# A state-space scan with top-1 experts on one core: the second layer of the rows beyond 256 with the weights standing still

## The chip, the cores and the metric

The kernel runs on one core of a Trainium2 chip. The metric is device time in microseconds of one execution, the median over runs. The engines are TensorE (PE, with its weight loads shown apart as PEld), VectorE (DVE), ScalarE (ACT), GpSimd (POOL) and SyncE (SP), which here only issues DMAs. "PEq" or "PEldq" is the sequencer of TensorE: it takes instructions in order and hands them to the array. TensorE multiplies a standing operand (lhsT, loaded by a weight load) with a moving one (rhs), and writes to PSUM.

## The reference

Two blocks in a row. The first is a chunked state-space scan (mamba2) over 4 batches x 8 heads x 768 steps; its output, seen as 3072 tokens x 256 features, goes to a mixture of 8 experts, one for each token:

```python
logits = x @ w_gate                      # x (3072, 256), w_gate (256, 8)
expert_idx = np.argmax(logits, axis=1)
probs = softmax(logits);  gate_w = probs[np.arange(N), expert_idx]
for e in range(8):
    mask = expert_idx == e
    h = np.maximum(x[mask] @ w1[e], 0.0)         # w1[e] (256, 1024)
    out[mask] = gate_w[mask, None] * (h @ w2[e]) # w2[e] (1024, 256)
```

Everything is float32. How many tokens an expert gets is known only at run time.

## The kernel before, in words

**Scan and placing (to about 65 us).** The scan makes a row of 320 numbers for each token (its 256 features, and parts of the gate's logits) and the token's number. GpSimd writes each row to a place of its own in `x_hbm`, a region of rows for each expert, with indirect DMAs (`place`, L434). The last group of 8 blocks of tokens is placed while the first expert jobs already run (`more_places`, L878).

**Jobs.** `jobs` (L479) is a list of pieces of expert work. Pass 0 is the first P1 = 256 rows of experts 0 to 3, pass 1 the next P2 = 192 rows of the same experts, pass 2 all 448 rows of experts 4 to 7. Rows that no token fills are zero and point to no token. `m_load` (L482) fetches a job's rows on the SP queue, four DMAs for the features and one or more for the rest of the row (`lt`, and `lh` for the half tile below). `m_xT` (L523) turns the features with a DVE transpose (`xT`, or `xTw` for pass 2) and works out the gate factors (`gates`, L502), which takes seven small DVE operations and one exponential on ACT between them.

**First layer.** `up` (L554) holds a 128x128 piece of w1 as the standing operand and moves the rows' features through it: 8 pieces f x 2 pieces t, n columns each, into one of four PSUM buffers `h_ps`. ACT applies ReLU and writes `hT` (1024 hidden features by rows; two such buffers).

**Second layer.** `m_y` (L589) works by tiles of 128 rows: the piece of `hT` is the standing operand and 256 columns of w2 move, 8 matmuls a tile, into one of two PSUM buffers `y_ps`. `put` (L575) multiplies by the gate (ACT for the first jobs, DVE from job 3 on) and GpSimd sends the 128 rows to their tokens in `out` with an indirect DMA (`send`, L570).

**Pairs.** Passes 1 and 2 run in pairs of experts (`m_pair`, L627). The number of rows n of a pair is known at run time: DVE counts the tokens (`over`, L451), and PE and ACT load the number of the size as a register (`number_of`, L619). `tc.Switch` (L634) then jumps to one of 17 programs, each written for one n: from 128 to 192 in steps of 4 for pass 1, from 320 to 448 in steps of 8 for pass 2. A program holds both experts' first layers, and `m_half` (L602): of the rows beyond 128 (pass 1) or 384 (pass 2), up to 64 of each expert side by side in one tile, 256 columns of w2 moving; where there are none, a product with zero on ACT. `tc.switch_hint` (L927, L942) tells the sequencers of PE and ACT ahead of time which program comes.

**Order.** It is written out by hand (`manual_schedule`): jobs 0 to 3, each first layer then second layer; then for each of four pairs the program, the hint for the next pair, the transposes and gates of the next pair, and the second layers of both. Weights of experts 0 to 2 have places of their own, 3 to 5 others that come free after the scan, and experts 6 and 7 take the places of 0 and 1. They are loaded on SP by `load_w` (L206) in quarters of 256 KB, at points of this order (`between`, `last_weights`, L883 and L934); two small DMAs (`go`, L599) make SP wait for a finished tile before it goes on to the later loads.

Of the kernel before, what the change touches and what calls it, by code (L numbers as in the profile page):

```python
# [41 lines left out]
MG = 7  # L42
PASS = ((0, P1, 2), (P1, P2, 1), (0, P1 + P2, 3))
WSIZES = list(range(P1 + FEW, P1 + P2 + 1, 8))
NR = N + 512
EW = 3
# [5 lines left out]
def ssd_then_moe(ctx, tc, xs_in, ae_in, wgx, w_gate, w1, w2, gx, gb, gc, ga, out):  # L52
# [42 lines left out]
    go = route.tile([1, 1], FP32, name="go")  # L95
# [68 lines left out]
    def empty_consts():  # L164
# [4 lines left out]
        for hT in hT_all:  # L169
            nc.gpsimd.memset(hT[:, :, WSIZES[0]:P1 + 128], 0.0)  # L170
# [308 lines left out]
    jobs = [(p, e) for p in range(2) for e in range(HE)] + [(2, e) for e in range(HE, E)]  # L479
    ex = [dict() for _ in jobs]  # L480

    def m_load(i, engs=(nc.sync,)):  # L482
# [4 lines left out]
        xb = mo.tile([128, (n if p == 2 else P1) // 32 * 64], FP32, name="xw" if p == 2 else "xb", bufs=2 if p == 2 else 4)  # L487
# [4 lines left out]
        lt = mo.tile([128, 3, MID], FP32, name="lt", bufs=7)[:, 0:tiles]  # L492
        nc.sync.dma_start(out=lt, in_=x_hbm[r0:r0 + 128 * tiles, DM:W].rearrange("(t p) w -> p t w", p=128))
        ex[i]["lt"] = lt
        if p and e % 2 == 0:
            lh = mo.tile([128, 1, MID], FP32, name="lh", bufs=3)
            for u in range(2):
                q = r0 + u * NR + 128 * tiles
                nc.sync.dma_start(out=lh[64 * u:64 * u + 64, 0], in_=x_hbm[q:q + 64, DM:W])
            ex[i]["lh"] = ex[i + 1]["lh"] = lh  # L500

    def gates(mids):  # L502

        ns = [m.shape[1] for m in mids]
        n = sum(ns)
        at = [sum(ns[:k]) for k in range(len(ns))]
        sh = [128, n, E]
        l = mo.tile([128, MG, E], FP32, name="t_l", bufs=2)[:, 0:n]
        for m, o, k in zip(mids, at, ns):
            logits(l[:, o:o + k], m)  # L510
        mx = mo.tile([128, MG], FP32, name="t_mx", bufs=2)[:, 0:n]
        nc.vector.tensor_reduce(mx, l, axis=AX, op=ALU.max)
        sub = mo.tile([128, MG, E], FP32, name="t_sub", bufs=2)[:, 0:n]
        nc.vector.tensor_tensor(out=sub, in0=l, in1=bc(mx[:, :, None], sh), op=ALU.subtract)
        nc.scalar.activation(sub, sub, func=ACT.Exp)  # L515
        se = mo.tile([128, MG], FP32, name="t_se", bufs=2)[:, 0:n]
        nc.vector.tensor_reduce(se, sub, axis=AX, op=ALU.add)  # L517
        nc.vector.tensor_scalar(out=se, in0=se, scalar1=1e-9, scalar2=None, op0=ALU.add)
        gt = mo.tile([128, MG], FP32, name="t_gt", bufs=5)[:, 0:n]
# [3 lines left out]
    def m_xT(i):  # L523
        p, e = jobs[i]
        n = PASS[p][1]
        for j in range(i, i + (2 if p else 1)):
            ex[j]["xT"] = (mo.tile([128, KT, n], FP32, name="xTw", bufs=2) if p == 2 else
                           mo.tile([128, KT, P1], FP32, name="xT", bufs=4))
            nc.vector.transpose(ex[j]["xT"][:, :, 0:n].rearrange("p k (r j) -> p k r j", j=32), ex[j]["xb"])  # L529
        if p:  # L530
            ex[i]["g"], ex[i + 1]["g"], ex[i]["gh"] = gates([ex[i]["lt"], ex[i + 1]["lt"], ex[i]["lh"]])
# [17 lines left out]

    def y_next():  # L550
        turn_no[1] += 1
        return Y[turn_no[1] % 2][:, 0:DM]
# [36 lines left out]
    def m_y(i, pp, then=None):  # L589
        e = jobs[i][1]  # L590
        for t in range(PASS[jobs[i][0]][2]):
# [5 lines left out]
            if then and (i < HE or t == 0):  # L597
                if i >= HE:
                    nc.sync.dma_start(out=go, in_=ex[i]["yo"][0:1, 0:1])  # L599
                then()  # L600
# [411 lines left out]
```

## Time and profile before

| what | us |
|---|---|
| median of 3 runs | 252.14 (251.94 to 254.53) |
| the profiled execution | 252.34 |
| its span, first to last instruction | 250.6 |
| PE busy | 237.7 |
| PEld busy | 185.7 |
| DVE, ACT, POOL busy | 82.5, 82.3, 75.4 |
| first-layer job of 256 rows on PE, start to start | 6.9 |
| second layer of one tile of 128 rows on PE | 3.45 |
| one half tile in a pair's program | 3.6 |
| one indirect send on POOL | 0.98 |

The difference between the profiled execution's own time and its span is what lies around the first and the last instruction. The granted TensorE clock is 0.999 throughout. In the rows of the profile, L558 is the first layer, L594 the second layer by tiles, L612 the half tile, L640 ReLU in a pair's program, L567 ReLU elsewhere, L578 the gate product on DVE, L571 the indirect send, L529 the transpose of a job's rows. A float32 matmul of the source appears as two matmul instructions, each with its weight load.

### The profile page before, as it was taken

The numbers are of one execution on the slowest core, as the hardware profiler recorded it, in microseconds if no ns is written. First come the engines' busy times: TensorE is split into PE (matmuls) and PEld (weight loads), VectorE is DVE, ScalarE is ACT, GpSimd is POOL, SyncE is SP. The second block draws the span as 40 slices with busy tenths as digits, with TensorE's granted clock in tenths as the row PEclk, the third lists the DMA queues.
The fourth block names the chain that finished last, engine by engine and source line by source line (L and its number), as shares of the span: only waits on it lengthen the run. The fifth ranks groups of instructions, "written<-read, shape, count | busy, mean of one in ns | idle before, by whom it ended". The sixth has DMA issues, their size and how long they took to land. (4 is left out here: it accounts for less than half of the span.)

```text
span 250.6 us, 5147 instructions
## 1 busy us (share of the span) xinstructions
PE 237.7 (95%) x1893; PEld 185.7 (74%) x1893; DVE 82.5 (33%) x220; ACT 82.3 (33%) x259; POOL 75.4 (30%) x129
## 2 busy tenths in 40 slices
PE   7898999987799999999999999999999999999992
PEld 4676877665588888888898978666788755558881
DVE  5897879677632123104121501010311100000110
ACT  4666657792131322324061431233300033420000
POOL 3664787673004833030113102100133200003331
PEclk9999999999999999999999999999999999999999
DMA  6999997724899437597971100640059600001101
GB/s 169 359 354 340 336 306 240 263 86 110 221 323 385 148 104 160 129 284 212 269 172 28 47 3 19 146 96 3 5 170 352 251 20 0 0 3 34 44 24 44
DMA packets 36363, 39.23 MB, mean 157 GB/s; under 512 B 21519, under 2 KB 24018, under 8 KB 36308
## 3 DMA queue, kind: packets, MB, share of 16 engines
q1 hardware_dynamic: 33156, 31.10, 41.6%
q0 software_dynamic: 2496, 7.28, 8.0%
q8 instruction: 27, 0.44, 0.8%
q10 hardware_dynamic: 656, 0.18, 0.3%
q14 instruction: 28, 0.23, 0.3%
HBM read 29.72 MB, written 9.35 MB: 156 GB/s over the span
## 5 line engine op out<-in xcount | busy, mean ns | idle before, releaser
L594 PE MATMUL y_ps<-w,hT 128*128 128x256 f32 x384 | 84.7, 380 | 0.0
L594 PEld LDWEIGHTS y_ps<-w,hT 128*128 128x128 f32 x384 | 72.6, 190 | 11.0 <-issue 0.8
L640 ACT ACTIVATE hT<-h_ps 128x128 f32<-128x128 f32 (+3 forms) x64 | 25.3, 395 | 66.5 <-PE h_ps L558 66.2
L558 PE MATMUL h_ps<-xT,w 128*128 128x256 f32 (+2 forms) x256 | 45.2, 335 | 1.2 <-DVE xT L529 1.2
L571 POOL DMA_INDIRECT out_dram<-yo,lt x24 | 23.7, 986 | 71.1 <-DVE yo L578 41.3
L558 PEld LDWEIGHTS h_ps<-xT,w 128*128 128x128 f32 x256 | 40.3, 190 | 4.9 <-DVE xT L529 1.5
L558 PE MATMUL h_ps<-xTw,w 128*128 128x368 f32 (+1 forms) x128 | 42.5, 492 | 0.0
L558 PEld LDWEIGHTS h_ps<-xTw,w 128*128 128x128 f32 x128 | 24.3, 190 | 17.4 <-issue 9.9
L578 DVE TENSOR_SCALAR yo<-y_ps,t_gt 128x256 f32<-128x256 f32 x18 | 8.7, 481 | 71.1 <-PE y_ps L594 71.1
L286 DVE TENSOR_TENSOR M<-g,mask 128x1024 f32<-128x1024 f32 x24 | 28.2, 1219 | 7.6 <-PE g L281 5.8
L425 POOL DMA_INDIRECT x_hbm<-rows,pos x24 | 23.9, 996 | 12.4 <-DVE pos L412 4.6
L571 POOL DMA_INDIRECT out_dram<-yh,lh x4 | 3.9, 984 | 62.1 <-ACT yh L614 36.6
L567 ACT ACTIVATE hT<-h_ps 128x256 f32<-128x256 f32 x32 | 12.1, 385 | 19.3 <-PE h_ps L558 12.9
L339 PE MATMUL y<-M,xp 128*32 128x128 f32 x384 | 15.5, 277 | 2.7 <-DVE M L286 2.2
L281 PE MATMUL g<-cm,xs_n 32*128 32x256 f32 x192 | 15.9, 405 | 1.3 <-issue 1.3
L517 DVE TENSOR_REDUCE t_se<-t_sub 128x2 f32<-128x16 f32 (+2 forms) x8 | 1.5, 182 | 44.2 <-ACT t_sub L515 44.2
L351 PE MATMUL r<-turn,yT 128*128 128x160 f32 x88 | 14.9, 312 | 1.2 <-ACT yT L344 1.0
L265 ACT ACTIVATE cm<-xs_n,par 128x128 f32<-128x128 f32 x46 | 15.1, 417 | 2.6 <-DMA xs_n<-in_xs_dram 2.5
L351 PEld LDWEIGHTS r<-turn,yT 128*128 128x128 f32 x88 | 12.2, 189 | 4.9 <-ACT yT L344 3.9
L344 ACT COPY yT<-y 128x512 f32<-128x512 f32 x12 | 7.0, 586 | 21.6 <-PE y L339 16.5
L275 POOL TENSOR_TENSOR xp<-xs_n,Ei 128x256 f32<-128x256 f32 x20 | 12.1, 619 | 5.4 <-DVE xp L275 3.4
L281 PEld LDWEIGHTS g<-cm,xs_n 32*128 32x128 f32 x192 | 9.5, 185 | 5.2 <-issue 4.8
(124 smaller groups left out, 149.7 us busy)
## 6 DMA issues: line engine op xcount, KB each, us to landing
w<-in_w_dram SPq DMA_DIRECT2D x64, 256.0 KB
xs_n<-in_xs_dram SPq DMA_DIRECT2D x20, 320.0 KB
xw<-x_hbm SPq DMA_DIRECT2D x16, 112.0 KB
x_hbm<-zrows SPq DMA_DIRECT2D x1, 1344.0 KB
xb<-x_hbm SPq DMA_DIRECT2D x14, 64.0 KB
xs_n<-in_xs_dram SPq DMA_DIRECT2D x4, 192.0 KB
xb<-x_hbm SPq DMA_DIRECT2D x16, 48.0 KB
xs_n<-in_xs_dram SPq DMA_DIRECT2D x4, 128.0 KB
```

Source lines behind the costliest of these rows:

```text
L265: nc.scalar.mul(t[:, u], st[n]["CT"], par[:, u:u + 1])
L275: eng.tensor_tensor(out=t, in0=st[n]["x"].rearrange("p (h d) -> p h d", d=D), in1=bc(Ei[:, n, :, None], [128, NH, D]), op=ALU.mult)
L281: nc.tensor.matmul(g_ps[:, q, n % 2], lhsT=st[n]["BT"][r], rhs=st[n]["cm"][r].rearrange("p u i -> p (u i)"), start=True, stop=True)
L286: nc.vector.tensor_tensor(out=t, in0=g_ps[:, :, n % 2].rearrange("p q (u i) -> p q u i", u=2), in1=bc(mask[:, None, None, :], [128, 4, 2, ...
L339: nc.tensor.matmul(y_ps[o:o + D, h // 4, CH * s:CH * s + CH], lhsT=st[n]["xp"][:, D * h:D * h + D], rhs=st[n]["M"][:, h], start=first, sto ...
L351: nc.tensor.matmul((to[s] if to else r_ps[:, s])[:, 256 * t:256 * t + 160], lhsT=sd[d]["yT"][:, t, CH * s:CH * s + CH], rhs=turn[:, t].rea ...
L425: s_ = nc.gpsimd.indirect_dma_start(out=x_hbm[:, :], out_offset=bass.IndirectOffsetOnAxis(ap=at, axis=0), in_=row, in_offset=None)
L558: nc.tensor.matmul(p[:, 0:n], lhsT=w[:, c:c + 128], rhs=xT[:, t, 0:n], start=(t == 0), stop=(t == KT - 1))
L567: nc.scalar.activation(ex[i]["hT"][:, f, 0:n], q, func=ACT.Relu)
L571: return nc.gpsimd.indirect_dma_start(out=out[:, :], out_offset=bass.IndirectOffsetOnAxis(ap=tok, axis=0), in_=yo[:, :], in_offset=None, b ...
L594: nc.tensor.matmul(p, lhsT=ex[i]["hT"][:, f, 128 * t:128 * t + 128], rhs=w_sb[e][1][:, f * DM:f * DM + DM], start=(f == 0), stop=(f == FT ...
L640: nc.scalar.activation(ex[i + u]["hT"][:, f, 0:n], q, func=ACT.Relu)
```

## The change

The rows beyond 256 get their second layer the other way round: a 128x128 piece of w2 stands (every second output column, so that a piece is 128 of the 256 features) and the n (pass 1) or n - 256 (pass 2) columns of `hT` move. This is done inside the pair's program (`m_rest`), so that n is exact, into a whole PSUM buffer for each expert. The result has features on partitions. `rest_out` turns it with DVE in blocks of 32x32, writes it to a table in memory with four DMAs an expert, and reads it back as two tiles of 96 rows; `rest_put` multiplies by the gate on GpSimd and sends them. The half tile, the zeroing of `hT` for it, and the pass 1 tiles are gone; pass 2 has two tiles by `m_y` instead of three. There is a third `hT` buffer. The jobs' order is new: (0,0), (0,1), (0,2), pair (1,0)+(1,1), the first layer of (0,3), pair (1,2)+(1,3), the second layer of (0,3), then the two pairs of pass 2. Loads, hints and weights are placed anew; the `go` DMAs are gone.

```diff
-PASS = ((0, P1, 2), (P1, P2, 1), (0, P1 + P2, 3))
+PASS = ((0, P1, 2), (P1, P2, 0), (0, P1 + P2, 2))
+REST = ((0, 0), (0, P2), (P1, P1 + P2))
+HP = P2 // 2
...
-        for hT in hT_all:
-            nc.gpsimd.memset(hT[:, :, WSIZES[0]:P1 + 128], 0.0)
...
+        if p:
+            lr = mo2.tile([HP, 2, MID], FP32, name="lr", bufs=6)
+            q = e * NR + P1
+            nc.sync.dma_start(out=lr, in_=x_hbm[q:q + P2, DM:W].rearrange("(t p) w -> p t w", p=HP))
...
+            if p == 2:
+                ex[i]["g"], ex[i + 1]["g"] = gates([ex[i]["lt"], ex[i + 1]["lt"]])
+            ex[i]["gr"], ex[i + 1]["gr"] = gates([ex[i]["lr"], ex[i + 1]["lr"]])
...
+    def m_rest(i, n):
+        p, e = jobs[i]
+        a = REST[p][0]
+        for f in range(2 * FT):
+            k, f = divmod(f, FT)
+            w = w_sb[e][1][:, f * DM:f * DM + DM].rearrange("p (m k) -> p k m", k=2)
+            nc.tensor.matmul(ex[i]["yr"][:, P2 * k:P2 * k + n - a], lhsT=w[:, k], rhs=ex[i]["hT"][:, f, a:n],
+                             start=(f == 0), stop=(f == FT - 1), skip_group_check=True)
+
+    def rest_out(i):
+        for j in range(i, i + 2):
+            t = mo2.tile([128, P2 // 32, 32, 2], FP32, name="rT", bufs=2)
+            nc.vector.transpose(t.rearrange("p r i k -> p k r i"),
+                                ex[j]["yr"][:, 0:2 * P2].rearrange("p (k r j) -> p k r j", k=2, j=32))
+            y = ys_hbm[jobs[j][1]]
+            for c in range(4):
+                nc.sync.dma_start(out=y[:, 64 * c:64 * c + 64].rearrange("(r j) z -> j r z", j=32),
+                                  in_=t[32 * c:32 * c + 32].rearrange("p r i k -> p r (i k)"))
+        for j in range(i, i + 2):
+            t = mo2.tile([HP, 2, DM], FP32, name="ys", bufs=2)
+            nc.sync.dma_start(out=t, in_=ys_hbm[jobs[j][1]].rearrange("(t p) w -> p t w", p=HP))
+            ex[j]["ys"] = t
+
+    def rest_put(i):
+        for j in range(i, i + 2):
+            for t in range(2):
+                yo = mo2.tile([HP, DM], FP32, name="yp", bufs=2)
+                nc.gpsimd.tensor_scalar(out=yo, in0=ex[j]["ys"][:, t], scalar1=ex[j]["gr"][:, t:t + 1], scalar2=None,
+                                        op0=ALU.mult)
+                put_out(yo, ex[j]["lr"][:, t])
...
             for u in range(2):
                 for f in range(FT):
                     q = up(ex[i + u]["xT"], w_sb[e + u][0], f, n, pp)
                     nc.scalar.activation(ex[i + u]["hT"][:, f, 0:n], q, func=ACT.Relu)
-            m_half(i, n, yo)
+            for u in range(2):
+                m_rest(i + u, n)
...
+        first(2)
+        hint(0)
+        m_y(2, pp)
+        m_xT(5)
+        m_pair(3, pp)
+        for j in (8, 9):
+            m_load(j)
+        rest_out(3)
+        first(5)
+        hint(1)
+        rest_put(3)
+        m_pair(6, pp)
+        hint(2)
+        rest_out(6)
+        m_xT(8)
+        m_y(5, pp)
+        rest_put(6)
+        m_pair(8, pp)
+        hint(3)
+        for j in (10, 11):
+            m_load(j)
+        m_xT(10)
+        rest_out(8)
+        for k in range(16):
+            load_w(E - 2 + k // 8, k % 8 // 4, k % 4)
+        m_y(8, pp)
+        rest_put(8)
+        m_y(9, pp)
+        m_pair(10, pp)
+        rest_out(10)
+        m_y(10, pp)
+        rest_put(10)
+        m_y(11, pp)
```

In the new list of jobs, 0 to 2 are (0,0) to (0,2), 3 and 4 are (1,0) and (1,1), 5 is (0,3), 6 and 7 are (1,2) and (1,3), and 8 to 11 are experts 4 to 7. The weights of expert 4 and half of expert 5's are loaded during job 1, before the rows of jobs 5 to 7, the other half of expert 5's during job 5.

## The prediction

> **What bounds the kernel now.** I read the page's busy table first, then PE in order of time, then the instructions at each jump, then the last microseconds of all engines.
>
> ```profile
> span 250.6 us, 5147 instructions
> PE 237.7 (95%) x1893; PEld 185.7 (74%) x1893; DVE 82.5 (33%) x220; ACT 82.3 (33%) x259; POOL 75.4 (30%) x129
> ```
>
> PE is the bound: no other engine passes a third. So the change is worth what it takes off PE's line, less any hole it makes there, less what it adds after PE's last matmul. PE from the third first-layer job on (start, length, line, shape, count):
>
> ```profile
> 110.68 7.07 PE L558 MATMUL h_ps<-xT,w 128*128 128x256 f32 x32
> 117.59 7.07 PE L594 MATMUL y_ps<-w,hT 128*128 128x256 f32 x32
> 124.49 7.31 PE L558 MATMUL h_ps<-xT,w 128*128 128x128 f32 x64
> 131.64 7.07 PE L594 MATMUL y_ps<-w,hT 128*128 128x256 f32 x32
> 138.56 9.16 PE L558 MATMUL h_ps<-xT,w 128*128 128x164 f32 x64
> 147.65 3.65 PE L612 MATMUL y_ps<-w,hT 128*36 128x256 f32 x32
> 151.23 7.17 PE L594 MATMUL y_ps<-w,hT 128*128 128x256 f32 x32
> 158.24 19.95 PE L558 MATMUL h_ps<-xTw,w 128*128 128x368 f32 x64
> 178.03 20.88 PE L594 MATMUL y_ps<-w,hT 128*128 128x256 f32 x96
> 198.75 22.51 PE L558 MATMUL h_ps<-xTw,w 128*128 128x416 f32 x64
> 221.19 3.65 PE L612 MATMUL y_ps<-w,hT 128*32 128x256 f32 x32
> 224.76 20.99 PE L594 MATMUL y_ps<-w,hT 128*128 128x256 f32 x96
> ```
>
> Each row starts where the one before stops: no holes, not even at the jumps. The shapes also tell which programs this data picks: n = 128, 164, 368, 416 for the four pairs; two pairs (128 and 368) have no 64-row half at all. A matmul in the source is two instructions (x32 for 16). I use start to start, since the lengths overlap: 7.15/64 = 0.1117 us for 128 columns, 9.09/64 = 0.1420 for 164, 19.79/64 = 0.3092 for 368, 22.44/64 = 0.3506 for 416, 6.91/32 = 0.216 for 256; a line of 0.00083 us a column.
>
> The jump into the second pair's program (PE's and ACT's hint, PE's jump, first instruction of the program):
>
> ```profile
> L942 PEldq BRANCH_PREFETCH_HINT  x1: 31/31/31, 131.4 to 131.4; - x1
> L942 ACTq BRANCH_PREFETCH_HINT  x1: 31/31/31, 134.8 to 134.8; - x1
> ...
> L1007 PEldq COMPARE_BRANCH  x2: 413/1929/3445, 130.4 to 135.0; - x2
> ...
> L634 ACTq BRANCH_PREFETCH_HINT  x1: 36/36/36, 137.8 to 137.8; - x1
> L634 PEldq BRANCH_PREFETCH_HINT  x1: 45/45/45, 138.5 to 138.5; - x1
> ```
>
> PE's jump at 135.0 took 3445 ns and the program began at 138.5, 7.0 us after the hint. It cost nothing because PE's sequencer was 3.6 us ahead of its array, whose next matmul was due at 138.56. It is a hidden stall with 0.1 us to spare.
>
> The end:
>
> ```profile
> 242.34 0.48 DVE L578 TENSOR_SCALAR yo<-y_ps,t_gt 128x256 f32<-128x256 f32 x1 [2.97 <-PE y_ps L594]
> 243.10 0.98 POOL L571 DMA_INDIRECT out_dram<-yo,lt  x1 [1.99 <-DVE yo L578]
> 245.79 0.48 DVE L578 TENSOR_SCALAR yo<-y_ps,t_gt 128x256 f32<-128x256 f32 x1 [2.97 <-PE y_ps L594]
> 246.55 0.98 POOL L571 DMA_INDIRECT out_dram<-yo,lt  x1 [2.47 <-DVEq L946]
> ```
>
> POOL is idle 2 us before each send, so the last send leaves at once: 0.76 us after the put starts, and the span ends 4.05 us after the send starts.
>
> **The change, part by part.** The profiled execution took 252.34 us, with a span of 250.6; the 1.7 around it I leave. The median of the three runs is 252.14, 0.2 below.
>
> *Matmuls removed.* Pairs 1 and 2 lose their 256-column second halves: 6.92 (131.64 to 138.56) and 7.01. Pairs 3 and 4 lose the third of three tiles: 20.72/3 = 6.91 and 6.90. The halves: 3.58 and 3.57. Sum 34.9 us.
>
> *Matmuls added.* 64 instructions a pair (2 experts x 8 x 2, doubled), of n columns in pairs 1 and 2, n - 256 in pairs 3 and 4: 128, 164, 112, 160. That is 64 x 0.1117 = 7.15, 64 x 0.1420 = 9.09, 64 x 0.1383 (the line at 160) = 8.85. For 112 the line says 0.0984, but its weight load is as large as in the 128-column row, where PEld is busy without a pause (7.10 of 7.10 us in that window), so I take that row: 7.15 (6.30 as the low end). Sum 32.2 us (31.4). **Net on PE: -2.65 us** (-3.5). Rows became columns, but only pairs 2 and 4 had much padding to lose.
>
> *The hint of pair 2.* It moves from in front of two y tiles (6.9 us) to directly in front of its own jump, behind job (0,3)'s up matmuls. In the trace the same code (third job's up, then hint) issues the hint at 115.3, when the array is 2.1 us from the end of that job; so PE hides 2.1 us of the wait. From hint to program PE took 7.0 us (131.4 to 138.5) and 6.5 us (149.8 to 156.4), but there the first fetch on the instruction queue (16 KB packets: 0.44 MB in 27) was not the hinted one: two fetches ran, at 132.4 and 135.9, 3.5 us apart, and the jump ended 1.3 us after the second. In the new place no jump has just been taken, so I take one fetch, 3.5 us: a hole of 1.4 us. ACT reaches its hint 0.8 us after the array ends the job (118.14 against 117.37) and needs 2.75 to 3.0 us (134.8 to 137.8): its first ReLU comes 3.85 us after, while PE, starting at 1.5, fills its four PSUM banks by 1.5 + 4 x 0.57 = 3.8 and waits 0.5 more for the first. **Together +2.1 us**; ends 0 and 7.0 - 2.1 = 4.9. The other hints keep 6.9 us or more of y matmuls in front of their jumps; the first pair picks its first program and its jump took 0.35 us.
>
> *Beside the matmuls.* A pair adds two DVE transposes (128x384: the same shape from SBUF takes 0.57 us), 8 writes and 2 reads on SP (0.44 us each to issue), 4 POOL products and 4 sends; it drops one tile or half a put each. Writes land about 2 us after issue (xb was issued by 93.8 and read at 95.8). The last read waits for the last writes: transpose, 2 us of issue, 2 to land, 0.5, 2: about 7.7 us after the pair. In the middle all this lies under 6.9 to 13.8 us of y matmuls. SP then holds 16 weight loads behind those reads: they start some 5.8 us after pair 3, issue in 10.5 us as now (183.28 to 193.8), and the first megabyte lands by 10, against 13.8 when pair 4 needs it: hidden, 4 us to spare. PSUM: the y bank of the first expert must be transposed before y begins; DVE was released in the middle of a pair's program (xTw at 168.34, when the first expert's ups ended), so it has the second expert's 3.6 to 4.5 us, of which after pair 3 about 5.5 of 7.15 us go to DVE's gates and transposes first. Hidden; if DVE were only released at the program's end, 0.9 us a pair for three pairs.
>
> *Order of jobs.* Pair 1 needs its size number, loaded at the same place as before, and rows that are issued at 94 to 99.4 and needed at 110. The 12 weight loads delay job (0,3)'s rows to about 112, needed at 124.8. The two POOL memsets that go (0.98 us at 14.3) had no PE instruction waiting.
>
> *The end.* Let T be the end of pair 4's program. PE runs 13.8 us more. POOL sends y tiles at T+4.5 and T+8.0, then must do four products and sends before the last two tiles' sends. A product of 96x256 is not in the trace: 0.24 to 0.30 us (POOL copies of 64 and 128 columns) below, 0.62 (a 128x256 product of two tensors) above; 0.45 from the slope of the copies. With 0.22 to start the send and 0.98: 1.65 each, so POOL is free at T+9.0+6.6 = 15.6, and the two sends start at T+15.9 and T+17.05. Unhindered the last starts at T+13.8+0.32+0.76 = 14.9. **+2.15 us** (1.2 if sends of 96 rows cost three quarters; 2.9 with the dear product).
>
> **Sum:** -2.65 + 2.1 + 2.15 = +1.6 on the profiled 252.34, or 253.7 from the median.
>
> [...]
>
> **Rivals.**
> 1. *Only the saving shows.* The hint's fetch is quick, the 96-row sends are short or POOL gets ahead: 252.1 - 2.65 = 249.5, with the 112-column end 248.6. For it: PE's jumps cost nothing at all four places. Against: at one of them by 0.1 us, with a lead that the change takes away. With one of the two costs paid, 251.6.
> 2. *Two fetches instead of one* (slower): 7.0 us from hint to program as at 131.4, a hole of 4.9: 256.5. It decides beyond 1% when the hole passes 3.1 us.
> 3. *Strided weights load slower* (slower): the new weights are every second column. Each of the 256 new instructions hides its load under 0.112 to 0.142 us. At 0.15 us a load it adds 128 x 0.038 + 64 x 0.008 + 64 x 0.012 = 6.1 us: 259.8; at twice 0.112 us, 279. It decides from 0.12 us. No weight load of this trace is strided; DVE reads xw at that stride without loss (896 columns in 1.1 us). [...]
>
> **How the numbers follow.** My forecast 0.45 (253.7, its own range 252.3 to 255.2); one cost paid 0.15; only the saving 0.10; two fetches 0.17; strided weights 0.08; DVE released late or the reads later than the products 0.05. About 1% (249.6 to 254.7) is what a measurement of this kernel tells from no change. Faster by more: the saving alone, 0.10. Slower by more: 0.17 + 0.08 + 0.05 and 0.05 of the forecast, 0.35. The rest, 0.55, is within. The range 250.0 to 257.0 leaves out the strided weights and most of the saving alone.
>
> **What would show it.** Right: PE's groups of 64 at 0.112, 0.142, 0.112 and 0.138 us; a hole of 1.5 to 2 us before the 164-column ups with a jump of some 3 us; POOL without idle time from T+8 on, and a last send 2 us behind its put. Wrong: a group of 112 columns above 0.12 us a piece (rival 3); no hole, or one of 5 us (1, 2); a hole before a y group (DVE late); PE waiting for w at pair 4.

## The result, and the profile after

The changed kernel takes 265.61 us (median of 6 runs, 263.11 to 267.31), the kernel before 252.04 us on the same chip (6 runs, 251.75 to 254.64). The ratio is 1.0477, 95% interval 1.0422 to 1.0533: slower by 4.8%. The prediction said 253.7, range 250.0 to 257.0: wrong, and far outside its range. The profiled execution took 267.03 us with a span of 265.3, against 252.34 and 250.6: 14.7 us more, and this is what has to be found. Executions of one kernel differ, and the ratios leave out those that run long, but the profiles of experiment 6 (253.44 us at a mean granted clock of 0.981, the others 249.41 to 252.97 at 0.981 to 0.987) and of experiment 10 (253.96 us at 0.980, the others 243.89 to 246.96 at 0.987 to 1.000) are of such ones.

The first lines of the page after:

```profile
span 265.3 us, 5332 instructions
PE 239.0 (90%) x1957; PEld 193.3 (73%) x1957; DVE 85.7 (32%) x230; ACT 80.9 (30%) x257; POOL 92.9 (35%) x147
```

PE is busy for 1.3 us more but for 5% less of the span: the time went into idle PE. Where, is read from PE in order of time (start, length, line, shape, count; in brackets the idle time in front and its releaser):

```profile
103.36 7.07 PE L600 MATMUL y_ps<-w,hT 128*128 128x256 f32 x32
110.27 7.31 PE L565 MATMUL h_ps<-xT,w 128*128 128x128 f32 x64
117.41 7.70 PE L613 MATMUL y_ps<-hT,w 128*128 128x128 f32 x64
127.47 7.14 PE L565 MATMUL h_ps<-xT,w 128*128 128x256 f32 x32 [2.35 <-DMA ys_hbm<-rT]
139.11 11.39 PE L565 MATMUL h_ps<-xT,w 128*128 128x164 f32 x64 [4.50 <-issue]
150.34 9.07 PE L613 MATMUL y_ps<-hT,w 128*128 128x164 f32 x64
159.72 7.16 PE L600 MATMUL y_ps<-w,hT 128*128 128x256 f32 x32 [0.32 <-issue]
167.94 20.02 PE L565 MATMUL h_ps<-xTw,w 128*128 128x368 f32 x64 [1.05 <-DMA xw<-x_hbm]
187.80 7.68 PE L613 MATMUL y_ps<-hT,w 128*128 128x112 f32 x64
196.31 14.07 PE L600 MATMUL y_ps<-w,hT 128*128 128x256 f32 x64 [0.83 <-DVE rT L620]
210.22 22.51 PE L565 MATMUL h_ps<-xTw,w 128*128 128x416 f32 x64
232.57 8.86 PE L613 MATMUL y_ps<-hT,w 128*128 128x160 f32 x64
241.26 14.02 PE L600 MATMUL y_ps<-w,hT 128*128 128x256 f32 x64
```

L565 is the first layer, L613 the new standing weights (`m_rest`), L600 the tiles of `m_y`. There are five holes where there was none. Rows without a hole overlap the next by 0.16 us (210.22 + 22.51 is 232.73, and the next starts at 232.57), so a hole is the bracket plus 0.16: 2.5 behind pair 1's program, 4.66 in front of pair 2's, 0.5 behind it, 1.2 in front of pair 3's, 1.0 behind it. Each stands at a jump of PE. The jumps there (duration in ns, start in us):

```profile
L1060 PEldq COMPARE_BRANCH  x1: 4446/4446/4446, 122.8 to 122.8; - x1
...
L1060 PEldq COMPARE_BRANCH  x1: 6279/6279/6279, 132.5 to 132.5; - x1
...
L1060 PEldq COMPARE_BRANCH  x1: 2355/2355/2355, 156.8 to 156.8; - x1
...
L1060 PEldq COMPARE_BRANCH  x1: 4546/4546/4546, 163.1 to 163.1; - x1
```

The first and third are jumps out of a program, which took 293 to 413 ns in the kernel before. The jump of 4446 ns ends at 127.3 and the next matmul starts at 127.47; the one of 6279 ns ends at 138.8, the next matmul starts at 139.11. So the releasers in the brackets ("DMA ys_hbm<-rT", "DMA xw", "DVE rT") are events that came before by chance: PE was at a jump, or at the hint's few instructions right behind one (0.5 to 0.6 us), with no lead left.

The 164-column ups also take 11.39 us where they took 9.16. The windows over that stretch (busy time and count of each engine, then PEclk, the granted clock, DMA share, GB/s):

```profile
127.00:137.00 10.00, 7.14 (x32) 6.00 (x32) 2.81 (x12) 3.30 (x10) 3.80 (x4) 0.99 0.56 168
137.00:144.00 7.00, 4.89 (x19) 4.92 (x20) 0.00 (x0) 1.01 (x4) 3.78 (x4) 0.52 0.12 35
144.00:148.00 4.00, 4.00 (x31) 4.00 (x30) 0.00 (x0) 2.26 (x8) 0.00 (x0) 1.00 0.00 0
```

From 137 to 144 the granted clock is 0.52 on average (0.5 from 136.9 to 143.7), at the end of the longest hole and behind it: 2.2 us more for the same matmuls.

The end, POOL from the last y tiles on:

```profile
249.17 0.98 POOL L578 DMA_INDIRECT out_dram<-yo,lt  x1 [2.48 <-DVE yo L585]
250.18 0.95 POOL L635 TENSOR_SCALAR yp<-ys,t_gt 96x256 f32<-96x256 f32 x1
251.41 0.96 POOL L578 DMA_INDIRECT out_dram<-yp,lr  x1 [0.28 <-POOL yp L635]
...
257.61 0.94 POOL L635 TENSOR_SCALAR yp<-ys,t_gt 96x256 f32<-96x256 f32 x1
258.83 0.95 POOL L578 DMA_INDIRECT out_dram<-yp,lr  x1 [0.28 <-POOL yp L635]
260.09 1.00 POOL L578 DMA_INDIRECT out_dram<-yo,lt  x1 [0.31 <-issue]
261.40 0.99 POOL L578 DMA_INDIRECT out_dram<-yo,lt  x1 [0.30 <-issue]
```

POOL is never idle for long (0.8 us at most): four products and four sends, of which two pairs are shown, take 250.18 to 260.09, 9.9 us, and the last send starts 5.6 us behind its gate product (DVE ended it at 255.80).

The account of the 14.7 us, forecast beside measurement:

| part | forecast | measured | from |
|---|---|---|---|
| PE up to the first pair | 0 | -0.4 | start at 110.27; before, after the same work, 110.68 |
| PE's matmuls, holes taken out | -2.65 | -2.1 | 145.0 us from there to PE's end (255.28) less 12.05 of holes and slow clock, against 135.1 |
| in front of pair 2 | +2.1 | +6.8 | hole 4.66, slow clock 2.2 |
| the other jumps | 0 | +5.2 | 2.5 + 0.5 + 1.2 + 1.0 |
| behind PE's last matmul | +2.15 | +5.2 | 265.3 - 255.28 = 10.0; before 250.6 - 245.75 = 4.85 |
| sum | +1.6 | +14.7 | |

### The profile page after: what moved, and what is told of

Read it like the earlier page. It is cut to its first block, busy times and chain, and to the rows that moved or that the text cites. A ratio compares the mean times of both kernels' runs of the same rounds, so it can differ in the third digit from the quotient of the medians.

```text
span 265.3 us, 5332 instructions
## 1 busy us (share of the span) xinstructions
PE 239.0 (90%) x1957; PEld 193.3 (73%) x1957; DVE 85.7 (32%) x230; ACT 80.9 (30%) x257; POOL 92.9 (35%) x147
## 4 chain that ended last, share of the span: by engine, by line
PE 37%; issue 27%; DMA 8%; POOL 8%; SPq 7%; DVE 7%; ACT 2%; POOLq 1%; another core or an unknown queue 1%; ACTq 0%; DVEq 0%
PE h_ps L565 13%; POOL out_dram L578 5%; PE y_ps L600 5%; DMA w<-in_w_dram 5%; SPq L490 4%; PE g L280 4%; PE r L350 4%; DVE M L285 4%; PE y L338 3%; PE y_ps L613 3%; POOL yp L635 3%; DMA xb<-x_hbm 1%; PE y L330 1%; DMA ys_hbm<-rT 1%; PE r L139 1%
## 5 line engine op out<-in xcount | busy, mean ns | idle before, releaser
L600 PE MATMUL y_ps<-w,hT 128*128 128x256 f32 x256 | 56.5, 380 | 1.1 <-DVE rT L620 0.8
L565 PE MATMUL h_ps<-xT,w 128*128 128x256 f32 (+2 forms) x256 | 47.5, 347 | 7.6 <-issue 4.5
L600 PEld LDWEIGHTS y_ps<-w,hT 128*128 128x128 f32 x256 | 48.3, 190 | 8.0 <-DVE rT L620 1.0
L565 PEld LDWEIGHTS h_ps<-xT,w 128*128 128x128 f32 x256 | 42.5, 200 | 11.6 <-issue 7.4
L578 POOL DMA_INDIRECT out_dram<-yo,lt x16 | 15.9, 992 | 98.6 <-DVE yo L585 77.2
L565 PE MATMUL h_ps<-xTw,w 128*128 128x368 f32 (+1 forms) x128 | 42.5, 493 | 1.1 <-DMA xw<-x_hbm 1.1
L565 PEld LDWEIGHTS h_ps<-xTw,w 128*128 128x128 f32 x128 | 24.2, 190 | 18.7 <-issue 11.3
L613 PEld LDWEIGHTS y_ps<-hT,w 128*128 128x128 f32 x256 | 33.1, 196 | 0.5 <-issue 0.3
L613 PE MATMUL y_ps<-hT,w 128*128 128x128 f32 (+3 forms) x256 | 33.3, 291 | 0.0
L620 DVE STREAM_TRANSPOSE rT<-y_ps 128x384 f32<-128x384 f32 x8 | 4.6, 579 | 65.9 <-PE y_ps L613 62.1
L635 POOL TENSOR_SCALAR yp<-ys,t_gt 96x256 f32<-96x256 f32 x16 | 15.1, 944 | 26.0 <-DMA ys<-ys_hbm 18.8
L578 POOL DMA_INDIRECT out_dram<-yp,lr x16 | 15.3, 957 | 5.0 <-POOL yp L635 4.4
L338 PEld LDWEIGHTS y<-M,xp 128*32 128x32 f32 x384 | 9.4, 109 | 6.3 <-DVE M L285 2.9
```

Of the source, the lines that this page charges most:

```text
L338: nc.tensor.matmul(y_ps[o:o + D, h // 4, CH * s:CH * s + CH], lhsT=st[n]["xp"][:, D * h:D * h + D], rhs=st[n]["M"][:, h], start=first, sto ...
L565: nc.tensor.matmul(p[:, 0:n], lhsT=w[:, c:c + 128], rhs=xT[:, t, 0:n], start=(t == 0), stop=(t == KT - 1))
L578: return nc.gpsimd.indirect_dma_start(out=out[:, :], out_offset=bass.IndirectOffsetOnAxis(ap=tok, axis=0), in_=yo[:, :], in_offset=None, b ...
L600: nc.tensor.matmul(p, lhsT=ex[i]["hT"][:, f, 128 * t:128 * t + 128], rhs=w_sb[e][1][:, f * DM:f * DM + DM], start=(f == 0), stop=(f == FT ...
L613: nc.tensor.matmul(ex[i]["yr"][:, P2 * k:P2 * k + n - a], lhsT=w[:, k], rhs=ex[i]["hT"][:, f, a:n], start=(f == 0), stop=(f == FT - 1), sk ...
L635: nc.gpsimd.tensor_scalar(out=yo, in0=ex[j]["ys"][:, t], scalar1=ex[j]["gr"][:, t:t + 1], scalar2=None, op0=ALU.mult)
```

## The experiments

Theory of the moment: a pair's program now has 256 matmul and load instructions on PE and some ten more, where the longest had 192 and these, and this length makes its jumps slow: the exit is no longer fetched when the jump comes, and the entry may need two fetches. That is supposed. The expectations take 256 instructions as the limit; what the runs show of it is that the jump out of programs of 128 to 240 matmul and load instructions took 0.3 to 0.4 us (once 0.9), out of those of 256 and 258 1.7 to 4.4 us. Rivals: the hint of pair 2 is given too late (the prediction's reason), and something that the new work itself waits for (the transposes, the writes to `ys_hbm`) makes the holes. The holes quoted are from start to start, as above. The experiments ran on three chips and are compared by their ratio to the kernel before on the same chip. PE's lead is the time by which its sequencer, when it reaches a jump, is ahead of the array's last work. The names in the expectations: e3_before_long is experiment 3, e6_all_mended experiment 7, e10_loads_first experiment 9.

**1. The hint earlier.** Only the place of one call is changed:

```diff
         m_pair(3, pp)
+        hint(1)
...
         first(5)
-        hint(1)
         rest_put(3)
```

> The changed kernel with one line moved: the hint of the second pair stands right behind the first pair's program, in front of job (0,3)'s first layer (6.9 us of matmuls). Theory 'late hint': PE's hole before the 164-column matmuls (4.66 us) goes nearly whole, since from hint to program it takes 6.5 to 8 us, and with it the slow clock in that stage (11.2 back to 9.1 us): 5 to 6.8 us off, about 259.5. Rival 'the jump itself is slow because the program is long': the jump into the second pair still takes 4 us or more with the hint 7 us ahead, and the hole stays over 3 us: above 262. Neither changes the jump out of the first pair (4.4 us now).

Measured: ratio 1.0352 (1.0279 to 1.0424). The hint was given at 128.8, 4.7 us ahead of its jump instead of 0.35, and the jump still took 5.6 us; from hint to program it was 10.3 us. The hole was 3.36 instead of 4.66, and no slow clock followed (1.00 from 134 to 146). But in experiment 4 below, where hint and jump stand as in the changed kernel, the jump took 5.2 us, the hole was 3.58 and no slow clock followed either (54 of the ups in 7.75 us, 0.144 each, against 64 in 9.15, 0.143, in this one and 64 in 11.39, 0.178, in the changed kernel): what this jump takes differs that much from one profile to the next, so that a gain by the early hint isn't shown at the jump itself. What is shown is that an early hint does not do what it is there for: the jump still takes 5.6 us.

**2. The program shorter.** The last four matmuls of the second expert (16 PE instructions) stand behind the switch, at a fixed width of 192 columns, so that the program has 240 matmul and load instructions:

```diff
-            for u in range(2):
-                m_rest(i + u, n)
+            m_rest(i, n)
+            m_rest(i + 1, n, range(2 * FT - 4))
+        m_rest(i + 1, REST[p][1], range(2 * FT - 4, 2 * FT))
```

> The changed kernel with the last 4 of the 64 float32 matmuls of each pair's program set behind it, at a fixed 192 columns: each program has 16 PE instructions fewer, so 243 to 250 instead of 259 to 266; hT is zeroed beyond the filled rows at the start on POOL. Theory 'a program over 256 instructions loses the prefetch of its exit': the jumps out of the pairs (4.4, 2.4, 2.4 and 2.3 us now) go back to 0.3, the holes behind pairs 1, 2 and 3 (2.5, 0.5, 1.0 us) and the one before pair 3 (1.2) go, the late hint's hole of 4.7 stays: 4 to 5 us off less 0.6 for wider columns, about 261.5. Rival 'the exits wait for something else (the new order, the y banks)': the exits stay at 2 us and more and the time at 265.

Measured: ratio 1.0294 (1.0211 to 1.0378). The jumps out of pairs 1 and 2 and the jump into pair 3, in this order:

```profile
L1064 PEldq COMPARE_BRANCH  x1: 316/316/316, 122.1 to 122.1; - x1
...
L1064 PEldq COMPARE_BRANCH  x1: 302/302/302, 152.7 to 152.7; - x1
...
L1064 PEldq COMPARE_BRANCH  x1: 391/391/391, 159.8 to 159.8; - x1
```

4446, 2355 and 4546 ns became 316, 302 and 391, and the four holes beside pair 2's entry are gone, with the transposes, the writes and the order as they were. That settles them: it was the length of the program, not the rest's own transfers. (At the entry of pair 3 the hint has more time by it: with the exit quick it stands 5.5 us ahead of the jump, from 154.3 to 159.8, instead of 3.5, from 159.6 to 163.1. In experiment 3 the jump into pair 3, a short program with its hint 3.5 us ahead, takes 3.6 us, so the hint's time fits and the length of the program that is entered does not.) The entry of pair 2 remains:

```profile
125.48 7.07 PE L567 MATMUL h_ps<-xT,w 128*128 128x256 f32 x32
134.53 2.46 PE L567 MATMUL h_ps<-xT,w 128*128 128x164 f32 x16 [1.99 <-issue]
138.93 8.62 PE L567 MATMUL h_ps<-xT,w 128*128 128x164 f32 x48 [1.93 <-ACT hT L666]
```

Its jump took 3837 ns instead of 6279, so the hole is 2.15. A second one of 2.1 stands inside the ups: PE fills its four banks and waits for ACT, whose program began only at 138.4, 5.2 us after ACT's hint. A stretch at a granted clock of 0.5 followed here too, from 139.7 to 143.1, behind two holes of 2.1 us each.

**3. The program longer, in the kernel before.** 33 tiny matmuls of 8 columns (66 PE instructions) at the start of each program; nothing else is touched:

```diff
             n = (SIZES, WSIZES)[p - 1][c]
+            for _ in range(33):
+                nc.tensor.matmul(H[(turn_no[0] + 1) % 4][:, 0:8], lhsT=ones_bf, rhs=ones_bf[:, 0:8], start=True, stop=True,
+                                 skip_group_check=True)
```

> The kernel before with 33 tiny bfloat16 matmuls of 8 columns (66 PE instructions) more in each pair's program, which do nothing for the result: 194 to 258 instructions and a few. Theory 'over 256 loses the exit': pairs 2 and 4 (258 and a few) leave by a jump of 2 to 4.5 us, pairs 1 and 3 (194 and a few, no half) by one of 0.3 us as now. Rival: all four stay at 0.3 us. The tiny matmuls themselves cost 1.5 to 4 us a pair.

Measured, in one run: the jumps out of the four programs, which have 194, 258, 194 and 258 matmul and load instructions, since only pairs 2 and 4 have a half tile:

```profile
L1010 PEldq COMPARE_BRANCH  x1: 303/303/303, 132.5 to 132.5; - x1
...
L1010 PEldq COMPARE_BRANCH  x1: 2171/2171/2171, 152.3 to 152.3; - x1
...
L1010 PEldq COMPARE_BRANCH  x1: 313/313/313, 178.7 to 178.7; - x1
...
L1010 PEldq COMPARE_BRANCH  x1: 3280/3280/3280, 228.3 to 228.3; - x1
```

In one and the same kernel the short programs leave in 0.3 us and the long ones in 2.2 and 3.3, with holes of 0.55 and 1.2 us behind them (4.13 and 4.79 us from the start of the half tile to the next row, against 3.58 and 3.57). The effect has nothing to do with the new second layer. The tiny matmuls themselves cost 0.83 us a pair, less than expected.

**4. The last pair's gate products on ACT.** Four buffers instead of two, and only for the last pair:

```diff
+                if i == 10:
+                    yo = mo2.tile([HP, DM], FP32, name="yq", bufs=4)
+                    nc.scalar.mul(yo, ex[j]["ys"][:, t], ex[j]["gr"][:, t:t + 1])
```

> The changed kernel with the four gate products of the last pair's rest on ACT (idle there) instead of POOL, with four buffers. Theory 'the products and their order on POOL set the end': 4 x 0.94 us and 0.3 us of waits go from POOL's line after PE's last matmul, 4 us off, about 261.5. Rival 'the end waits for the rows to come back from memory': ys lands too late for ACT to be ahead of POOL, and under 1.5 us go.

Measured: ratio 1.031 (1.0216 to 1.0405). The last sends of that profile:

```profile
249.32 0.92 POOL L578 DMA_INDIRECT out_dram<-yq,lr  x1 [0.30 <-issue]
250.54 0.99 POOL L578 DMA_INDIRECT out_dram<-yo,lt  x1 [0.30 <-issue]
251.83 0.99 POOL L578 DMA_INDIRECT out_dram<-yo,lt  x1 [0.30 <-issue]
```

A product takes ACT 0.46 us, POOL now only sends, every 1.22 to 1.29 us, and the span ends 5.3 us behind PE's last matmul (250.47) instead of 10.0. The tail was POOL's products.

**5. The hint late in the kernel before.** It is moved from behind the first pair's program to directly in front of its jump, behind the two y jobs:

```diff
-                tc.switch_hint(chosen(k + 1), len(SIZES), f"pair{k + 1}")
+                if k > 0:
+                    tc.switch_hint(chosen(k + 1), len(SIZES), f"pair{k + 1}")
...
             m_y(i + 1, pp)
+            if k == 0:
+                tc.switch_hint(chosen(1), len(SIZES), "pair1")
```

> The kernel before with one line moved: the hint of the second pair stands directly in front of its jump, behind both y tiles, instead of 6.9 us ahead; its programs stay under 256 instructions. Theory 'one fetch takes 4.2 us when nothing else is fetched' (as in the short-program run): PE's sequencer is 3.6 us ahead there, less 0.5 us for the hint's own instructions, so PE gets a hole of 1 to 1.5 us, and ACT, 5 us from hint to program, another 1 to 2 us: 2 to 3.5 us slower than before, about 254.5. Rival 'a late hint alone makes the changed kernel's hole': a hole of 4.5 us or more and the slow clock behind it, 258 or more.

Measured: ratio 1.0042 (1.0007 to 1.0077). The hint came 0.36 us ahead of the jump, and the jump took as long as with the hint 3.5 us ahead: 3427 ns against 3445. From hint to program it was 3.8 us, where the prediction had taken 3.5 for one fetch; the hole was 0.63, and ACT had none. So the kernel became 1.0 us slower, half of the least that was expected, and the rival is out: a late hint alone does not make a jump of 6.3 us. In the kernel before, too, the early hint of this pair had gained nothing; what hid the jump was PE's lead.

**6. Hint early and program short together.** The edits of experiments 1 and 2.

> The changed kernel with both edits: programs 16 PE instructions shorter, and the second pair's hint behind the first pair's program. Theory 'the early hint failed because the long program's exit had used up its lead': now the exit takes 0.3 us, the hint is 7 us ahead and the jump finds its program; the hole before the 164-column matmuls and ACT's wait inside them (4.2 us together in the short-program run, and 1.6 us of slow clock) go: about 255. Rival 'a hint ahead of other code is lost': PE's jump still takes 4 us or more, time 259 to 260.

Measured: ratio 1.0224 (1.0138 to 1.031). The jump out took 316 ns, the hint came at 119.0, the jump at 125.4 and took 4530 ns, the hole was 2.30. ACT, whose hint now came in time, had no hole any more. So a short program does not make PE's early hint work; that the jump still takes over 4 us is what the rival had said. Why the hint is lost is not shown by this.

**7. All three edits, and the last pair's sends between the two tiles of expert 6.**

> The changed kernel with the short program, the early hint, the last pair's gate products on ACT and its four sends of the rest between the two tiles of expert 6. If exits, hint and POOL's end are the whole loss, PE's last matmul comes at 244 to 244.5 us of the span (245.5 in the kernel before), the end 5 us later: 250 to 251.5 us, up to 1% below the kernel before. If something else also costs, 253 or more.

Measured: ratio 0.9976 (0.9925 to 1.0028), no difference from the kernel before. The tail ends 4.9 us behind PE's end, as before the change; the entry of pair 2 still has a jump of 3877 ns and a hole of 1.65.

**8. Weights with unit step.** The 128 columns of a piece of w2 are neighbours, and POOL's product takes two tensors. The kernel leaves the features of the rows beyond 256 in another order, so it stands for these two prices alone:

```diff
-.rearrange("p (m k) -> p k m", k=2)
+.rearrange("p (k m) -> p k m", k=2)
...
-                nc.gpsimd.tensor_scalar(out=yo, in0=ex[j]["ys"][:, t], scalar1=ex[j]["gr"][:, t:t + 1], scalar2=None,
-                                        op0=ALU.mult)
+                nc.gpsimd.tensor_tensor(out=yo, in0=ex[j]["ys"][:, t], in1=bc(ex[j]["gr"][:, t:t + 1], [HP, DM]), op=ALU.mult)
```

> A look at two prices in the changed kernel: the standing pieces of w2 are 128 neighbouring columns instead of every second one (so the features of the rows beyond 256 come out in another order), and the gate product on POOL is the two-tensor form with a broadcast factor. If the step of two costs the weight load its 6 ns, the 128- and 112-column groups go from 0.118 to 0.112 us a matmul; if the 112-column group falls to 0.098, the load is not the floor. The POOL product is expected at 0.6 us (the two-tensor row of the kernel before) against 0.94.

Measured, in one run. PE's groups of 128 and of 112 columns:

```profile
110.60 7.31 PE L613 MATMUL y_ps<-hT,w 128*128 128x128 f32 x64
...
178.74 7.29 PE L613 MATMUL y_ps<-hT,w 128*128 128x112 f32 x64
```

and POOL's product:

```profile
L635 POOL TENSOR_TENSOR yp<-ys,t_gt 96x256 f32<-96x256 f32 x16 | 10.0, 624 | 30.2 <-DVE t_l L371 19.4 <-DMA out_dram<-yp,lr 10.7
```

7.31 and 7.29 us with unit step, 7.70 and 7.68 with a step of two: 0.39 over 64 instructions, 6 ns each, 0.8 us in the whole kernel. In the changed kernel PE's weight loads with a step of two take 196 ns each, those with unit step 190, by PEld's rows. And 112 columns take as long as 128 in both forms, while PEld is busy nearly without a pause (7.40 of 7.50 us in the changed kernel's group of 112), so the weight load is the floor, as the prediction had taken it from the 128-column row. The same product, given as two tensors, takes POOL 624 ns instead of 944.

**9. The register loads in front of the hint.** In experiments 1, 6 and 7 three registers (the sizes of pairs 3 and 4, and a flag) are loaded between the early hint and its jump. Experiment 7 with these loads moved to job 2:

```diff
-            if i == 5:
-                for k in range(2, 4):
-                    number_of(k)
...
-                for k in range(2):
+                for k in range(4):
                     number_of(k)
```

> e6_all_mended with one change: the registers for the sizes of pairs 3 and 4 and for the general path are loaded in job 2, beside those of pairs 1 and 2, so that no register load stands between the early hint of pair 2 and its jump. Theory A (a register load between hint and jump makes the early hint worthless; in every profile so far the jumps of 0.3 to 0.4 us had none between): the jump into pair 2 falls from 3.9 to 0.3-0.5 us, the hole before the 164-column ups from 1.65 to under 0.3 us, the ratio to the kernel before from 0.998 to about 0.992. Theory B (the hint is lost to the code of job (0,3) itself, whose instructions take the place of the fetched page, or because it is given right behind a jump): the jump stays at 3.4 to 4.6 us, the hole at 1.5 to 2.3, the ratio at 0.995 to 1.003.

Measured: ratio 0.9925 (0.9874 to 0.9975), faster than the kernel before. The jump into pair 2, and the rows around it:

```profile
L1066 PEldq COMPARE_BRANCH  x1: 389/389/389, 123.8 to 123.8; - x1
```

```profile
111.43 8.07 PE L615 MATMUL y_ps<-hT,w 128*128 128x128 f32 x64
119.33 16.09 PE L567 MATMUL h_ps<-xT,w 128*128 128x256 f32 x96
135.26 9.26 PE L615 MATMUL y_ps<-hT,w 128*128 128x164 f32 x64
```

The jump is down from 3877 to 389 ns, and there is no idle time left: the second row holds job (0,3)'s ups and those of pair 2 in one, because nothing lies between them. But the jump into pair 1 became slow, in experiment 7 and here:

```profile
L1068 PEldq COMPARE_BRANCH  x1: 446/446/446, 102.2 to 102.2; - x1
...
L1066 PEldq COMPARE_BRANCH  x1: 3197/3197/3197, 100.7 to 100.7; - x1
```

Between that hint and its jump nothing changed: 64 matmul and load instructions, no register load, 5.5 and 5.65 us. The 3.2 us cost nothing, because the jump stands behind two y tiles, where PE's lead is 3.2. So the wait was not only mended at pair 2; one of its kind appeared where it is covered. And the intervals of experiments 7 and 9 overlap, so the gain between the two is read from the traces, not from the times.

**10. A y tile in front of the jump.** Experiment 7 with the second tile of job 2 kept back until behind job (0,3), and the hint in front of that tile:

```diff
-        m_y(2, pp)
+        m_y(2, pp, ts=(0,))
...
         first(5)
+        hint(1)
+        m_y(2, pp, ts=(1,))
```

> e6_all_mended with one change: the second y tile of job 2 stands between the ups of job (0,3) and the jump into pair 2, with the hint in front of it (hT buffer of job 2 kept until then, its gate product on DVE). Theory (what hides the jump is the lead of PE's sequencer over the array: 3.6 us behind y tiles, which wait for nothing, against 1.6 to 2.3 us behind ups, which wait for PSUM banks): the jump takes 0.4 us if the hint is taken and 3.4 to 3.9 us if it is not, in both cases under or near the lead, so the hole before the 164-column ups is 0 to 0.5 us, against 1.65; ratio to the kernel before 0.990 to 0.994. Rival (the lead is the same whatever stands in front, and the jump is simply late): hole 1.5 to 2.3, ratio 0.998 as for e6_all_mended. A second rival: pair 1, now with one tile in front of it, opens a hole of its own of 1 us or more.

Measured: ratio 0.996 (0.9909 to 1.0011), so no difference that is clear of noise, and less than expected. In the profiled execution the hole at pair 2 is gone as expected (the jump, reached at 132.05, took 1550 ns), but as the second rival has it pair 1, now with one tile in front of its jump, had a jump of 6902 ns and a hole:

```profile
99.94 3.62 PE L604 MATMUL y_ps<-w,hT 128*128 128x256 f32 x16
107.97 9.56 PE L567 MATMUL h_ps<-xT,w 128*128 128x128 f32 x64 [4.42 <-issue]
```

Here the cover was moved, not made; one profile does not show how often that is so.

**11. One register load put back** (that of the flag), into experiment 9's kernel:

> e10_loads_first with one of the three register loads (that of the general path) put back into job (0,3), between the early hint of pair 2 and its jump. Theory A (a register load itself undoes the hint): one is enough, the jump into pair 2 goes from 0.39 back to 3.4 to 4.6 us and a hole of 1.5 to 2.3 us stands before the 164-column ups. Theory A' (it is the number of instructions between hint and jump, and the three loads with theirs were just too many): the jump stays at 0.3 to 0.5 us and there is no hole.

**12. More code, no register load.** Experiment 9's kernel with 24 tiny matmuls between hint and jump:

```diff
+                for _ in range(24):
+                    nc.tensor.matmul(H[(turn_no[0] + 1) % 4][:, 0:8], lhsT=ones_bf, rhs=ones_bf[:, 0:8], start=True,
+                                     stop=True, skip_group_check=True)
                 m_xT(6)
```

> e10_loads_first with 24 tiny bf16 matmuls (8 columns; 48 instructions with their weight loads, about 0.6 us together by the 0.83 us of 33 in e3_before_long) in job (0,3), between the early hint of pair 2 and its jump, and no register load there. Theory A (only the register load undoes the hint): the jump into pair 2 stays at 0.3 to 0.5 us, no hole before the 164-column ups. Theory A' (the number of instructions between does it): the jump takes 3.4 to 4.6 us, hole 1.5 to 2.3 us.

Measured, one run each. The jump into pair 2 with one load:

```profile
L1066 PEldq COMPARE_BRANCH  x1: 1444/1444/1444, 133.9 to 133.9; - x1
```

and with the tiny matmuls:

```profile
L1069 PEldq COMPARE_BRANCH  x1: 4208/4208/4208, 129.9 to 129.9; - x1
```

With no register load in between and 48 more instructions, the jump is as slow as before experiment 9 (hole 1.94); with one load it took 1.4 us (no hole, since the lead covers it), which neither theory had expected. So the reason given in experiment 9, that a register load undoes the hint, falls: it is not needed. Nor does the number of instructions decide: the hint of pair 4 has 128 or 192 of them behind it in every kernel here, and its jump took 0.3 us in all. And single jumps scatter: the one into pair 1 took 3197 ns in experiment 9 and 1222 in experiment 12, with the same code up to it, and 451 in the changed kernel and 2291 in experiment 1, again with the same code up to it. One profile each can't tell what a load or 48 instructions cost.

What the traces do show is the packets of the instruction queue; those of 16 KB are taken here as PE's. In experiment 9 two were fetched ahead of the jump into pair 2 (at 117.9 and 121.1, the hint at 117.3, the jump at 123.8). In experiment 11 also two, the second later (127.9 and 132.7, the hint at 127.5, the jump at 133.9). In experiment 12 only one (123.3, the hint at 122.8), and the next at 131.1, behind the jump's arrival at 129.9. So a quick jump had its second packet early, and a slow one waited for it. All 56 jumps into programs in the 14 profiles, by how far ahead of the jump PE's hint stood:

| hint ahead of the jump, us | jumps | the jump took, us |
|---|---|---|
| 10.4 to 20.5 (pair 4 in every kernel) | 14 | 0.3 in all |
| 5.5 to 7.1 | 25 | 0.3 to 0.45 in 17; 1.2 to 4.5 in 8 |
| 0.35 to 4.8 | 17 | 0.9 to 6.9 |

What decides in the middle row stays open: the time at which the second packet is fetched is seen, its reason is not, and the profile does not say which code a packet brought.

## Why the prediction was wrong

**The step that failed** is one that the sum does not have: the jumps out of the programs, and those into them apart from pair 2's, stand there with 0. Experiments 2 and 3 show from both sides what the longer programs cost at them: out of programs of 128 to 240 matmul and load instructions a jump takes 0.3 to 0.4 us (37 of 38 jumps in the profiles; once 0.9, in experiment 5), out of those of 256 and 258 it takes 1.7 to 4.4 us (all 18). With the entry of pair 3, which the short program also mended, it is 5.2 us of holes at four places, where the sum has 0. For the entry the prediction had written "The other hints keep 6.9 us or more of y matmuls in front of their jumps"; of the exits it says nothing. That the programs grow from 192 to 256 such instructions could be counted; a cost that no row showed was set to nothing, where the rows had a price to bound it by: the jump of 3.4 us at 135.0, up to eight times, less PE's lead of 0 to 3.6 us each time.

**The hint of pair 2**, forecast as +2.1 ("In the new place no jump has just been taken, so I take one fetch, 3.5 us: a hole of 1.4 us"), was +6.8. With 3.5 us the step is nearly right: experiment 5 has 3.8 us from hint to program, experiment 2 has 4.25 and a hole of 2.15. That the packet at 132.4 in the kernel before was not the hinted one is the prediction's reading; the trace shows the packets' times, not which code they brought. The changed kernel had 6.75 us and a hole of 4.66, close to the end of 4.9 that belonged to rival 2 (two fetches, 256.5 us). That is luck: only one 16 KB packet of the instruction queue lies between hint and program, at 136.3, 3.8 us behind the jump's arrival, where in experiment 2 it came 1.4 us behind. That the longer program makes the difference between 6.3 and 3.8 us of jump is what experiment 2 suggests, and with the hint as late the other two long kernels took 5.2 and 5.5 us (experiments 4 and 8), the other short one 3.4 (experiment 5). It isn't settled, since a jump into a short program took 6.9 us once (experiment 10, pair 1), and in experiment 3 the one into the long program of pair 2 took 3.8, hardly more than the 3.6 into the short one of pair 3. ACT, forecast at 0.5 us, cost 2.1 in experiment 2. And nothing in the sum allowed for the clock: 2.2 us behind the hole.

**The end**, forecast as +2.15, was +5.2, and experiment 4 shows that POOL's products are the reason. The mechanism was right (POOL without a pause, products and sends in one row), its size was not: a product took 0.944 us, not 0.45 and not even the upper bound of 0.62, and four products with their sends 9.9 us instead of 6.6; 2.0 of these 3.3 us are the products, the rest pauses between them and the sends. The bound came from a product of two tensors (L275); experiment 8 shows that this form indeed takes 0.624, but the kernel uses the form with one factor for each partition.

**What held.** The saving on PE is real: -2.1 us against -2.65; the strided loads, 0.8 us, are more than the difference. Their rival (3) had the right sign and a price six times too high for the lowest case it worked out, 38 ns against 6 in experiment 8. The pitches: start to start 0.139 us for 164 columns (forecast 0.142), 0.136 for 160 (0.138), 0.118 for 128 and 112 instead of 0.112. Weights, transposes and reads were hidden as forecast: with the short program no hole stands where they are needed.

**Where the gain went.** Taken out one after another: the program shortened to 240 matmul and load instructions and the hint of ACT and PE early, the tail's products off POOL and its sends between the tiles (experiment 7), the register loads ahead of pair 1's hint (experiment 9), which left no hole at any jump. What is left is 0.75% (0.25 to 1.3%) faster than the kernel before. From the end of job (0,2) to its last matmul PE takes 133.7 us in experiment 9 (104.28 to 237.99) and 135.1 in the kernel before (110.68 to 245.75), for the same tokens. So the new second layer does bring its saving; the change gave it back several times over by the size of its programs, by the wait at one entry and by one engine's tail. Why a hint that is given in good time is sometimes lost stays open.

## What to carry to other kernels

Before a program behind a run-time jump is made longer, count its instructions on PE, weight loads included, and price the exit and the entry as waits that nothing hides if the count passes that of the longest program whose jumps a trace shows to be quick (192 here in the kernel before; then 240 left by a quick jump and 256 by a slow one); the nearest slow jump in the trace has the price, and what stands in front of the jump says how much of it is covered. A hint is worth what the trace shows at its jump, so look at the jump's duration and not at the hint's place: here hints 10.4 us or more ahead of their jumps worked 14 times of 14, those 5.5 to 7.1 us ahead 17 times of 25, and those 4.8 us or less ahead in none of 17. Look at every jump after each edit, and at more than one profile: a wait that left one place turned up at another, and the same code gave 0.45 us once and 2.3 us once. When a product moves to another engine at the end of a kernel, take its time there from the same operation with the same kind of factor, not from a like shape (on POOL 0.944 us with one factor for each partition, 0.624 with a tensor).

## What the runs showed of the hardware

- A jump on PE out of a program took 0.3 to 0.4 us (once 0.9) where the program has 128 to 240 matmul and load instructions, and 1.7 to 4.4 us where it has 256 or 258; in experiment 3 both stand in one kernel.
- A jump on PE into a program took 0.3 to 0.45 us where the hint had worked, and 0.9 to 6.9 us where it had not or not in time; hints 10.4 us or more ahead worked in all 14 cases, those 4.8 us or less ahead in none of 17.
- What hides such a jump is PE's lead: 3.6 us behind y tiles in the kernel before (at 135.0) and 3.0 in experiment 5, but 1.9 to 2.5 us behind ups, each piece of which needs a PSUM bank that ACT has emptied (experiments 2 and 7: reached at 130.4 and 125.2, the array's work there ended at 132.4 and 127.7).
- The clock: with holes of 3.95 us (experiment 8), 4.58 (experiment 10) and 4.66 us (the changed kernel) the granted clock was 0.5 for 3.4 to 6.8 us; behind single holes of up to 3.58 us (experiments 1, 4, 6, 7, 12) it was not. These runs set no single length as the limit, since 3.58 us did not do it and behind two holes of 2.1 us, with 2.5 us of matmuls between them, it was 0.5 for 3.4 us (experiment 2). In the changed kernel it cost 2.2 us on top of the hole.
- A float32 weight load of 128x128 with a step of two columns takes 196 ns, with unit step 190 (both in the changed kernel); matmuls of 112 and 128 columns behind them start every 0.118 us instead of 0.112 (experiment 8).
- POOL multiplies 96x256 float32 by one factor for each partition in 0.944 us (the changed kernel), by a tensor in 0.624 (experiment 8); ACT does the former in 0.46 (experiment 4).
